# Chunk-selected attention with a gated MLP: score strips by query halves, PSUM tiles in pairs, dummy matmuls at the start, a new order table

## The chip, the core and the metric

The kernel runs on one core of one Trainium2 chip. A core has five queues of instructions that the profile names: PE (TensorE, matmuls; PEld are its weight loads), ACT (ScalarE), DVE (VectorE), POOL (GpSimd) and SP (SyncE, which issues transfers). Each queue is worked off in the order of the program, and queues wait for each other through semaphores. The metric is the time of one execution in device microseconds (us), given as the median of three runs.

## What is computed

The inputs are q, k and v (4 batches, 8 heads, 768 positions, 64 wide) and four weights of an MLP. Each query may look only at the 6 chunks of 32 keys with the largest upper bound of their scores, and only backwards.

```python
def _attn_ref(q, k, v):
    B, H, S, D = q.shape                       # 4, 8, 768, 64
    chunk = 32; nc = S // chunk; top_k = 6; scale = 1.0 / np.sqrt(D)
    k_chunks = k.reshape(B, H, nc, chunk, D)
    k_min = np.min(k_chunks, axis=3); k_max = np.max(k_chunks, axis=3)
    ub = np.sum(np.maximum(q[:, :, :, None, :] * k_min[:, :, None, :, :],
                           q[:, :, :, None, :] * k_max[:, :, None, :, :]), axis=-1)
    ub = np.where(causal, ub, -1000000000.0)
    top_chunks = np.argsort(ub, axis=-1)[..., -top_k:]
    scores = scale * np.matmul(q, k.transpose(0, 1, 3, 2))
    mask = sel & (pos[:, None] >= pos[None, :])
    scores = np.where(mask, scores, -1000000000.0)
    attn = np.exp(scores - np.max(scores, axis=-1, keepdims=True))
    attn = attn / (np.sum(attn, axis=-1, keepdims=True) + 1e-09)
    return np.matmul(attn, v)

def _moe_ref(x, w_in, w_spatial, b_spatial, w_out):   # x: (4, 768, 512)
    h = np.maximum(x @ w_in, 0.0)
    u, v = h[..., :512], h[..., 512:]
    v_n = (v - mean(v)) / np.sqrt(var(v) + 1e-06)
    v_s = np.einsum('ts,bsd->btd', w_spatial, v_n) + b_spatial[None, :, None]
    return (u * v_s) @ w_out
```

## The kernel before

**Units of work.** Two heads make a pair, and there are 16 pairs, four to a batch. A batch's MLP can begin when its four pairs are done. The 768 positions are six tiles of 128.

**A pair.** `load_ops` (L356) brings k, q and v; most loads are issued by POOL, which also turns them from f32 to f16 (L370), and some may go through SP into an f32 stage and a cast on an engine (L376). `prep_ops` (L431) turns k on PE (L440) or by a transfer (L443) into `kT`, takes minima and maxima per chunk on DVE (L449 to L455), turns q (L477), computes the bounds (`ub`, L489), picks the sixth largest (MAX8, L505) and writes the unselected chunks as extra rows beside q (`select`, L511). The result `qs` is turned into `a` by a transfer (L516) or on PE (L525). The extra rows of `kh` hold a large negative number, so one matmul gives scores with the chunk mask in them. The first pair has a path of its own, one head at a time (`prep_first`, L532: L545, L579, L590, L603, L616).

**Attention of a pair** (`attend_ops`, L623). Scores are computed transposed, keys by queries, in strips: for each key tile the queries from its diagonal on. `STRIPS` (L22) packs the 21 blocks of 128 by 128 of one head into six strips, five 512 wide and one 128 wide. Each strip takes a PSUM tile, PE fills it (L641), and ACT takes the exponential into `e` (L651). The three diagonal blocks of each half of the strips need a triangle set to zero: either PE adds a matrix of large negative numbers before the exponential (L644), or POOL clears them after it (L659). Then PE multiplies by v with a column of ones (L667), and DVE divides by the sum (L675, L679) into `x16`, which is turned into `xT` by a transfer (L687) or on PE (L694).

**The MLP of a batch** (`mlp_ops`, L700). Per tile of positions: four matmuls for v (L713), a ReLU, statistics and the normalisation on DVE (L719 to L730); four matmuls for u (L740) and a ReLU; six matmuls with the spatial weight (L754), a DVE instruction that adds the bias `bcol` and multiplies by u (L758) into `g`; `g` turned by a transfer (L762) or on PE (L768); four matmuls with `w_out` (L775), a copy into `o` (L240 on ACT or L244 on DVE) and a store (L780).

**What sets the order.** Operations are not issued in the order of the source. `Schedule.run` (L153) reads the string `PLAN` (L49): three digits name an operation, and the third also holds the engine, where an operation has several (`EVAC`, `RELU`, `KH` and so on), and which of eight PSUM tiles it takes. The table was found by a search outside the program; only its result is here. So one sequence holds the instructions of all engines, and each engine gets its share of it in this order. The semaphore waits are put in by the framework, from the tiles that each instruction reads and writes. The eight PSUM tiles are made one by one:

```python
    banks = [pp.tile([P, 512], F32, name=f"bank{j}") for j in range(8)]
    s = Schedule(banks, {"sc": 3, "tr": 2, "ub": 1, "av": 2, "mlp": 4})
```

Of the kernel before, what the change touches and what calls it, by code (L numbers as in the profile page):

```python
# [8 lines left out]
F32 = mybir.dt.float32  # L9
# [5 lines left out]
P = 128  # L15
# [5 lines left out]

STRIPS = [  # L22
    [(0, 0, 512, 0)],
    [(1, 128, 512, 0)],
    [(2, 256, 512, 0)],
    [(0, 512, 256, 0), (4, 512, 256, 256)],
    [(1, 640, 128, 0), (3, 384, 384, 128)],
    [(5, 640, 128, 0)],
]
WIDTHS = [512, 512, 512, 512, 512, 128]  # L30
BASES = [0, 512, 1024, 1536, 2048, 2560]
EW = 2688
DIAGS = [(0, 512), (1792, 384)]


def blocks(groups):
    out = []
    for g in groups:
        for (t, q0, n, col) in STRIPS[g]:
            for j in range(n // P):  # L40
                out.append((t, q0 // P + j, BASES[g] + col + j * P))
    return out
# [7 lines left out]
    "0700b00400000600100D00C00B00k00I00M00P00800c10J00H00500O10e00f10r40s10h00A00N11A82I00K10G00L10E0"  # L50
    "0l10Q01B03o00u00t01MC0w01D01010y00+11F03t02YG1C01H01J10i11E01N00302Z13w00v01L11G01O011K1K01I142O"
    "0200x00z11302o21205I02Q02N02b01PS0/114W4311Q08q00W02l12d00m04G11R05Y4AK05Q01504501S02c01602n21T8"
    "4JC2m24F24I25N05Z12pG1U12e017018K4601wO25S22W2f04702g02k04802h15b05c01z42r14A01912882j02701/02i0"
    "4902q00V01YK1tG4C02sS2A04L04E01g44B04D04K01v02401jC1a04M80X01l05e01VG2t01X05g02T01y01bW2u04N02v0"
    "4O094K2zS2xC2+01mG0F05d00R04P021O5f02y01d02C02D01i03TS4H19515pW5r03Y88y04T435C1o05h14RK3V04U03a0"
    "5q03GG8v09803I04S02/S9A03703Q42E03S05k05885i05j05sG5t09709C032W3104wCBq01fK5u03z09904y03N45A05v0"
    "52O5l16yS3P05406z01q03AC6q8AS05543406r03C04zO4/05700T05zG1r09B03bW3d05+04gS4i06oCAa85o11s03eO5x4"
    "3XG4jW3g04mK5n16bS5m15y1Ab0AP04o06p05T02F04l09LOAe03D84tC6e4Ad03i09E03F039K9N09D26QWAf06g00U03K0"
    "4v09G09F0DK09M09K16d09J14V8Ag09I14YOAh09H13j0Ai09O46YC3k06S04X0C4S6a03L09P06AG51W5C06C03M04a06NK"
    "9Q06T86P0ArC5/G6V05D0As19R09V45E06GOC509TW9W062K6I0Al0At0Aj065S6s8C804b49U0Am0Ap1Ak0AuCCA0610Av0"  # L60
    "6706XO3l06i04d0A5G6DWAw06409bS4f44q06j0Ax00S06F069KC704r0A8CAq19zW6t0A609c06K09+09YGDa8An19Z04s0"
    "9wSBv0By0A909e49f06k06L0Ao16uWC907IO78G9mCCC06M0Db09x0Ay09n0De05GKCB0CJ15H16m4CK16n0A0873S6+CDP0"
    "Gg0CL4CG2CF26v0A107906/0IA07J0CI0CE2CM1Dg0CH1700CN0ABK740Di07SWCD1Gl0CO8BG47K07T0750DS0Dd0Df07A0"
    "9jC090710AC0BDOCP0720BH08/0CQ09k07cS9pG7B0Jg07d0BeKBE09q06w4Bf0CR0760GwC7e0AV0B887C07NO7fG6x0B90"
    "7707U0BJKBK07O0Bb4Bc0CS0Dh0AD07L0Gx0Dl29g0Dn1Dj2B2SB307D07g07h07P1Dr8Go07iWDk10Y0BTKDs09r0BQCBR0"
    "9h4BhOBi07j0Dt0A20B5S7Q0BW87V0Dq1Dm0DuG7E07k19s09t0Gz09u07F0Dv07W0A3CAE0Dw0IF0Dp1CmOAF0BU07R0Do1"
    "CjKB60Dx07M07G0II0G/0CYW7rSBX0Cn0IS0D84Ck0AG07l87m0DV0H71BL0CbO7s0BA0CpKCZ07oWBj07n0CeG7H0H91DB8"
    "Cc07X07Y0DC07t07p0Dy0HA1Cf0Cq0BBOBM0BY0AICHB87q07b0H10CwSB/08MGHC07uKH81AJ17Z0BZWG+07a00Z0Bk0Jy0"
    "8N0H00BN0Jo07v0H20HD1Bl0H60BO0D5CD90H317w07x0Cx0D08IU0H40Cz4EGS82OH50If1Cg0Bm0Cr0D60D10E8CC+0D20"
    "HEKHF0E908O0Ih8LA0HG0EH0E548CWE60IW08D0Ij1HH0E2C8E0EWSE30Jl0Ii0IT0EJ4EK0Ig18F0EeKIV0Ef0Ch8EQCED4"  # L70
    "EhWDD0HI0EE0Cs08P0BoKIY0830IX0EX0OW0Ct0840Ib0ETG8W4ER0J+0IZ0EbSEU0Ia1Ic1Ei0Id2Ec0K00850Bp1D3CDE0"
    "Jz0DF0IkGIl0LQW8X07y0EA0EBOJ/0DG0Im0K208Q0EL0EM0KBSIn0LI08Y0Cu0Ie1LR1EN0860K108gCKC1EO0HZKLU0Io0"
    "8h0Ha0HsWHt0DIGEY0Hm8Hn08i0Ej0EZOKA1HUKEk0I1WHV0LF0K50RW0LT0KD1DJ1K718Z0Ev8Ob0K42I20K61K928a0K30"
    "El0Em0LV07/4OmKLW0HcOEoS8j0LY0Hd0Gr0Ep0K81HpGLX0Lc0KEC8TWE+SHfOE/0On0Ew0Oq0FIKHq0IL0F00FJ0Lb0Ex0"
    "Oe0KF08U0KG0FDGF10800FE0Op0LhSFK0JR8HOWHg0Ey0HR4EqKHP0Er0HS0F20J3OKH0JUCH+WIu4FF1La0Es1Q00JJGJ40"
    "Ez0FVKKI0Et0JV0Hh0810Iv0FW0H/0Li0Ld1JS0FX0FbOFc0Lj0LZ0HxCHu0Hy0Eu0Q80JX4JK0FL0Os0Ou0JY0IxSOr0LkW"
    "Iy08d8FG0FhKLe18G0Fi0Lf0J9CJA0Ll0Ot0Jr0F30JMGF84HW0F90J6SLg1JN0Lm0HXCHi0Ow2T00I30Fj1FA1HvGJGKFH0"
    "Hj08e0Ln0Ov2FB0F40F50K+8QI0I40J70JZ0Rb0P14P20P30Hk0Oy1Fd0I+W8JSJH0O/189OO+1Lo0Oz18A1K/0FC0P01Ro0"
    "FM0F60Ox0I508K0Re0JO0I/0KcKL18Kp4KmSL20J00Kd0P4CFYWKq0I60Kf8KxOFZ0FSKP50Kn0KO4Fa1FT0FeGKy0KP08k0"
    "KRSQ50P60P70JB0KZOJPWF70FU08B0Ja0Jb0Kg0FN0Ka0Jc0Ks4MGKFO0L+8Kt0KS0FkCFf0Fg0MROLuWMS0J14FQ0MH0JC0"  # L80
    "KUSFP0Fl0M9GGCOFR0LxKGD0KV0Ku0QU1P80QJ0L/0Kh0QV1Fm0I70LL0QK0MUSKW0JD0MM8Rp0JE0Rq0Fn0GE0MA0L30Lv0"
    "QL0MN0QM0QN0Fo0GF0Rr0Rs0MV0MX4MY0Jd0M3GQT1MZ0M6WFuCKv8L40KXSL50T50M70PE4PF0QO0PfOFv0MJWL60Fw0Ly0"
    "Fx0Rt0M40Oh08n88o1Fy0QX4Ki0Kj0PiKS02QZ0GMGMK0M00QY1PSCPPWQQ0QP1GN0QW1Kk0M18Pg0PT0T80PV4PW0Ru0TI0"
    "PHOPI0PtSQS0MB0GO0MC0MD0ME08L0L70PqCPK4Pu0QR1Pj0GP0MO0MPOMa0PL0GWSRx2QaKPn8G24Pr0Rw2M+GPcCMb0Po0"
    "Pd0Mc0Md0Pv0N8OGX0GY0S18Qb0G30G40Qc0Qd0S30TK0TV18V0Rv2Pk0Qe0PQ0Ry1GZ0FrCRh0MlKFs0TJ0S20TXWTY0MqS"
    "S48MgCM/0TM0S50TL0S60TZ1R/2Mh0N00TN0S70QB0TO0TP0TS0Mm0Mn1Mo0Mi0N90NA1F/WNXGPX0NY08p0S80GG0Qq8TU2"
    "TQ1G00Mp0QnCG50Mj0Qr0Mr0GQ0TR0Ms0QyKQz0PlWG10TaOTb0Qk8Mt0Tc0Td0Q/4Pw0Px0Mu0NZ0TT1TE0NLSQo0PM0Mk0"
    "NIKN3GN40N51N60Ql0RCCRD0NJ0R+2N70RN8RO0NK1G60R00NM0QvONN0PNCQs0Mv0PY0Py0Qw0SfGGJ8Sg0St4Su0ScSNUK"
    "GK1R6OGa0Rz0Te0Sd0N10NV0NRWNS0GL0TF0Mw0My0R70TC0SKGR10Ft0PZ0Pa0SP8SS4SQ0SL0SnSSo0NW1NOONP0SECSF0"
    "RK8NQ1RHGR9KQtSNB0RI0R20GTOSiCR30N20RA0Mx0R40SqGRL0GdKRE0NC0Sr0ND0Sj0RP0G98ST0GU18f0NE0Ge1TnSTo0"  # L90
    "GA0SVGMz0NF0RFOTqCOMKTW1U64SW0SHSSI0NT1RQ0Tr0Na8SM0Nb0TkGTl0Ts0UCWTySU70NkCUD0Nl0NG0Sk0NH0Pz0Nc0"
    "U9GTz0Sv0T/4RR0RS0Nm0UA0UNOSX0Nn0NuWRT0Nd0No0U00SNSSY0SZ0TD0UKGUL0UO0Ne0UH4SlCSw0Sa0Nv0Tv8O2GUI0"
    "UP0Sx0Sy0Tw0Sz0ON0OO0U10Nw0TtOVNSU20U30U40Gf0UE0UF4UQ0UR0US0Nx0Ny0NrCNs0OP0UW8O30UUOUg4UV1UqCUvW"
    "O40Uh0O50UbKU+OUi1U/0V00Uj0Uk0UX0VBGV10V20Nt0UY0Uc0UZ0GB0Uw0Ux1VH4VI0Ud0Ue0Ur0Us0Uf0Ua0Ut0Uu0Uy0"
    "VJ0VKOUl0VO0Um0VP0OC8NhKUz0O60Ni0V8WUn0N/CUo0OQ0V30V40V60V90OD0GV0V70V50VL0O94OA1VC0OB0VuSVQKOE0"
    "VE4O00VA0O10Up0Vv0VR0VS0OF0VT0OTCVD0VM0VaWVb0Vc0Vd0Nj0Vw0VkGOG0VF0Vl0Vx0OU0Vm0VU0OV0Ve0OJOVG1Vn0"
    "W28W30Vy0W40WCKWD0WE0VhCW50WF0OK0Vo0OL0VXWW60WHSV/4Vi0WI0Vj0VrGVY0W00VZ0W10Vs0Vt0WJOWK0WL0W98WA0"
    "WB0"
# [3 lines left out]
class Bank:  # L102
    def __init__(self, cls):
        self.cls, self.tile = cls, None
# [14 lines left out]
class Schedule:  # L119
# [3 lines left out]
    def __init__(self, banks, caps):  # L123
        self.ops, self.banks, self.caps = [], banks, caps
        self.keys, self.mode = {}, {}

    def op(self, alts, emit, key, r=(), w=(), take=None, drop=None, load=0.0, tag="", when=None, after=()):
# [66 lines left out]
def kernel(  # L194
# [40 lines left out]
    banks = [pp.tile([P, 512], F32, name=f"bank{j}") for j in range(8)]  # L235
    s = Schedule(banks, {"sc": 3, "tr": 2, "ub": 1, "av": 2, "mlp": 4})
# [34 lines left out]
    bcol = cp.tile([P, NQT], F32, name="bcol")  # L271
    w_in_sb = cp.tile([P, NDO, DFF], F16, name="w_in")
# [7 lines left out]
    stage_r = ring(8, [P, NQT, D], F32, "stage")  # L280
# [10 lines left out]
    e_r = ring(4, [P, EW], F16, "e")  # L291
    rec_r = ring(4, [P, NQT, 1], F32, "rec")
    x_r = ring(3, [P, NQT, 2, D], F16, "x16")
    xT_r = ring(3, [P, NDO, S], F16, "xT")
    vr_r = ring(11, [P, DH], F32, "vraw")
# [7 lines left out]
    o_r = ring(4, [P, DM], F32, "o")  # L303

    nc.scalar.preload_act_table_set("natural_log_exp_and_others")
# [9 lines left out]

    def preset(qs):
        nc.vector.memset(qs[:, :, 0, 0:D], 0.0)
        nc.vector.memset(qs[:, :, 1, D:P], 0.0)

    def const_ops():  # L320
        s.op(("DVE", 0.1, 0.2), lambda: nc.vector.memset(identity, 0.0), -100, w=["identity"])
# [21 lines left out]
        for j in range(len(kh_r)):  # L343
            for hi in range(2):
                s.op([("ACT", 0.72, 0.87), ("DVE", 0.45, 0.58)], lambda e, j=j, hi=hi: copy(
                    e, kh_r[j][D * hi:D * hi + D, hi, :], ex, False), -40 + 10 * j, r=["ex"], w=[("exrow", j, hi)])
        s.op(("SP", 0.45, 2.5), lambda: nc.sync.dma_start(out=bcol, in_=moe_b_spatial.rearrange("(t p) -> p t", p=P)),
             20, w=["bcol"])

    def both(qs):  # L350
# [479 lines left out]
```

## Time and profile before

| | |
|---|---|
| three runs | 197.38, 198.13, 1056.44 us |
| median | 198.13 us |
| the profiled execution | 195.9 us |
| its span, first to last instruction | 194.2 us |
| busy DVE, ACT, POOL | 158.4 (82%), 147.9 (76%), 118.5 us (61%) |
| first matmul of a score strip (L641) | starts at 16.00 us |
| last matmul (L775) | ends at 190.5 us |
| transposes by transfer | `gT` 23, `a` 11, `xT` 9, `kT` 5 |

The profiled execution is the one that durations are taken from. One of the three runs is far from the other two, and the median is not moved by it. A row of a group in the profile gives the line, the engine, the operation, output and input tiles with their shapes, the count, the busy time with the mean duration of one in ns, and the engine's idle time just before such instructions with what ended it. Matmuls follow each other in a pipeline: the mean duration of one includes the time until its result is written, and the time from one to the next is shorter. A busy PE is therefore not yet a PE at its peak.

### The profile page before, as it was taken

How to read it: one execution, taken by the hardware profiler on the slowest of the kernel's cores; microseconds unless marked ns; L12 is line 12 of the kernel's file. 1: busy time of each engine (PE TensorE's matmuls, PEld its weight loads, DVE VectorE, ACT ScalarE, POOL GpSimd, SP SyncE). 2: the span in 40 equal slices, each digit the busy share in tenths (PEclk: the TensorE clock that was granted, in tenths of full speed). 3: DMA queues.
4: the chain of work that ended last, by engine and by line, in shares of the span. 5: the costliest groups of instructions: out<-in, count | busy, mean ns of one | idle time of the engine just before them, and what ended most of it. 6: DMA issues, size and time to landing. Idle time of an engine off the chain costs nothing.

```text
span 194.2 us, 5292 instructions
## 1 busy us (share of the span) xinstructions
PE 181.0 (93%) x1888; PEld 112.8 (58%) x1888; DVE 158.4 (82%) x568; ACT 147.9 (76%) x317; POOL 118.5 (61%) x207
## 2 busy tenths in 40 slices
PE   0579999999998999999999999999999999999992
PEld 0367888776664657565566566555565664444440
DVE  8799999896999889998999986799889436973620
ACT  7799999989997999778989978667888722652142
POOL 7699999989999998697976785523223530000000
PEclk9999999999999999999999999999999999999999
DMA  6999999999999999999999999799994264406565
GB/s 133 137 160 171 192 167 146 137 149 171 155 155 168 125 119 175 124 172 146 201 139 150 203 108 150 187 142 222 149 265 65 41 149 137 110 0 199 139 203 216
DMA packets 122457, 29.50 MB, mean 152 GB/s; under 512 B 117056, under 2 KB 119360, under 8 KB 122432
## 3 DMA queue, kind: packets, MB, share of 16 engines
q0 software_dynamic: 72528, 11.60, 89.3%
q1 hardware_dynamic: 49904, 17.57, 48.6%
q8 instruction: 14, 0.23, 0.5%
q14 instruction: 11, 0.09, 0.2%
HBM read 24.38 MB, written 6.29 MB: 158 GB/s over the span
## 4 chain that ended last, share of the span: by engine, by line
PE 68%; DMA 12%; DVE 7%; ACT 5%; POOL 4%; issue 2%; SPq 1%; ACTq 0%; POOLq 0%; DVEq 0%
PE bank L754 13%; PE bank L641 13%; PE bank L775 10%; PE bank L740 9%; PE bank L713 8%; PE bank L667 7%; DMA a<-qs 4%; DMA qs<-in_q_dram 3%; DMA kp<-in_k_dram 3%; ACT e L651 2%; DMA stage<-in_k_dram 2%; PE bank L477 2%; DVE m L505 1%; PE bank L489 1%; DVE kmm L455 1%
## 5 line engine op out<-in xcount | busy, mean ns | idle before, releaser
L651 ACT ACTIVATE e<-bank 128x512 f16<-128x512 f32 (+1 forms) x192 | 92.4, 559 | 12.5 <-PE bank L641 9.8
L641 PE MATMUL bank<-a,kh 128*128 128x512 f16 (+3 forms) x256 | 56.1, 305 | 0.7 <-DMA a<-qs 0.7
L659 POOL TENSOR_SCALAR_AFFINE_SELECT e<-e 128x384 f16<-128x384 f16 x48 | 25.6, 550 | 22.0 <-ACT e L651 21.0
L754 PE MATMUL bank<-vn,wsT 128*128 128x512 f16 x144 | 38.0, 379 | 0.0
L641 PEld LDWEIGHTS <-kh 128*128 128x128 f16 x256 | 22.7, 97 | 15.8 <-DMA a<-qs 0.8
L667 PEld LDWEIGHTS <-e 128*128 128x128 f16 x672 | 25.4, 97 | 5.0 <-issue 0.3
L667 PE MATMUL bank<-vt,e 128*128 128x65 f16 x672 | 27.2, 193 | 0.2 <-ACT e L651 0.2
L242 POOL COPY kh<-kT 64x384 f16<-64x384 f16 x46 | 24.0, 522 | 3.7 <-PE bank L641 1.5
L758 DVE SCALAR_TENSOR_TENSOR g<-bank,bcol,u 128x512 f16<-128x512 f32 x24 | 17.6, 745 | 10.2 <-PE bank L754 10.0
L740 PE MATMUL bank<-w_in,xT 128*128 128x512 f16 x96 | 25.9, 379 | 0.0
L370 POOL DMA_DIRECT2D qs<-in_q_dram x30 | 25.1, 840 | 0.0
L713 PE MATMUL bank<-w_in,xT 128*128 128x512 f16 x96 | 24.4, 379 | 0.0
L240 ACT COPY o<-bank 128x512 f32<-128x512 f32 x18 | 10.4, 587 | 18.3 <-PE bank L775 18.3
L775 PE MATMUL bank<-w_out,gT 128*128 128x512 f16 x96 | 23.6, 379 | 0.0
L754 PEld LDWEIGHTS <-wsT 128*128 128x128 f16 x144 | 13.4, 98 | 12.1
L679 DVE TENSOR_TENSOR x<-bank,rec 128x384 f16<-128x384 f32 x32 | 17.5, 549 | 0.4
L370 POOL DMA_DIRECT2D kp<-in_k_dram x15 | 15.5, 1032 | 2.1 <-ACT qs L240 1.5
L719 DVE BATCH_NORM_STATS2 st<-vraw 128x6 f32<-128x512 f32 x24 | 16.3, 684 | 0.4
L370 POOL DMA_DIRECT2D vt<-in_v_dram x15 | 15.3, 1023 | 0.0
L775 PEld LDWEIGHTS <-gT 128*128 128x128 f16 x96 | 9.1, 98 | 9.7
L713 PEld LDWEIGHTS <-xT 128*128 128x128 f16 x96 | 9.0, 98 | 9.0
L740 PEld LDWEIGHTS <-xT 128*128 128x128 f16 x96 | 8.9, 98 | 8.5
(90 smaller groups left out, 280.0 us busy)
## 6 DMA issues: line engine op xcount, KB each, us to landing
out_dram<-o SPq DMA_DIRECT2D x24, 256.0 KB, 2.3
kp<-in_k_dram POOLq DMA_DIRECT2D x15, 192.0 KB, 6.1
qs<-in_q_dram POOLq DMA_DIRECT2D x30, 96.0 KB, 5.5
vt<-in_v_dram POOLq DMA_DIRECT2D x15, 192.0 KB, 6.5
ws_raw<-in_moe_w_spatial_dram POOLq DMA_DIRECT2D x3, 384.0 KB, 6.5
w_in<-in_moe_w_in_dram POOLq DMA_DIRECT2D x4, 256.0 KB, 7.8
w_out<-in_moe_w_out_dram POOLq DMA_DIRECT2D x2, 256.0 KB, 6.1
stage<-in_k_dram SPq DMA_DIRECT2D x2, 192.0 KB, 3.4
```

What stands on the lines that cost most here:

```text
L242: nc.gpsimd.tensor_copy(o, f)
L370: s.op(("POOL", cost, 0), lambda: nc.gpsimd.dma_start(out=o[0] if len(o) == 1 else o[2], in_=f[0] if len(f) == 1 else f[2]), key, w=w, loa ...
L641: mm(bs.f32[:, col:col + n], lhsT=kh[:, hi, t * P:(t + 1) * P], rhs=af[:, q0 // P:(q0 + n) // P, :], start=True, stop=not dg)
L651: s.op(("ACT", *act_cost(WIDTHS[g])), lambda g=g, bs=bs, e=e: nc.scalar.activation(out=e[:, BASES[g]:BASES[g] + WIDTHS[g]], in_=bs.f32[:, ...
L659: nc.gpsimd.affine_select(out=o, in_=o, compare_op=Alu.is_ge, fill=0.0, base=0, channel_multiplier=-1, pattern=[[0, 3], [1, P]])
L667: mm(o[:, qi, :], lhsT=e[:, c:c + P], rhs=vt[:, hi, t, 0:D + 1], start=(part == 0 and n == 0), stop=(part == 1 and n == len(bl) - 1))
L679: nc.vector.tensor_tensor(x16[:, :, hi, :], in0=o[:, :, 0:D], in1=rec.to_broadcast([P, NQT, D]), op=Alu.mult)
L713: mm(bk.f32, lhsT=x[:, ko, t * P:(t + 1) * P], rhs=w_in_sb[:, ko, DH:DFF], start=(ko == 0), stop=(ko == NDO - 1))
L740: mm(bk.f32, lhsT=x[:, ko, t * P:(t + 1) * P], rhs=w_in_sb[:, ko, 0:DH], start=(ko == 0), stop=(ko == NDO - 1))
L754: mm(bk.f32, lhsT=wsT[:, si, t * P:(t + 1) * P], rhs=vn[:, si, :], start=(si == 0), stop=(si == NQT - 1))
L758: s.op(("DVE", 0.67, 0.80), lambda t=t, bk=bk, g=g: nc.vector.scalar_tensor_tensor(out=g, in0=bk.f32, scalar=bcol[:, t:t + 1], in1=u_r[nu[ ...
L775: mm(bo.f32, lhsT=gT[:, db, :], rhs=w_out_sb[:, db, :], start=(db == 0), stop=(db == KO - 1))
```

## The change

The line numbers on the plus side are those of the changed kernel (`score` L672, triangle on PE L675, exponential L683, triangle by minimum on DVE L692 or POOL L694, multiplication with v L703, MLP L752, L779, L793, L797, L807, L814).

**PSUM tiles.** Four tiles of 1024 columns are made in place of eight of 512, and the eight entries that the table hands out are their halves:

```diff
-    banks = [pp.tile([P, 512], F32, name=f"bank{j}") for j in range(8)]
-    s = Schedule(banks, {"sc": 3, "tr": 2, "ub": 1, "av": 2, "mlp": 4})
+    double = [pp.tile([P, 1024], F32, name=f"bank{j}") for j in range(4)]
+    banks = [double[j // 2][:, 512 * (j % 2):512 * (j % 2) + 512] for j in range(8)]
+    s = Schedule(banks, double, {"sc": 3, "tr": 2, "ub": 1, "av": 2, "mlp": 4})
```

**Dummy matmuls.** A tile of zeros is multiplied with itself, 31 times and then three times 5; the groups are tied in before the first head's and the second head's transposes:

```diff
+        s.op(("DVE", 0.08, 0.15), lambda: nc.vector.memset(warm, 0.0), -102, w=["warm"])
+        for j in range(NWARM):
+            bw = Bank("tr")
+            def spin(n=31 if j == 0 else 5, bw=bw):
+                for _ in range(n):
+                    nc.tensor.matmul(bw.f32[:, 0:P], lhsT=warm, rhs=warm, start=True, stop=True)
```

**Score strips.** The 21 blocks of a head are packed so that strips 0 and 1 hold the queries of tiles 0 to 2, and strips 2 to 5 those of tiles 3 to 5. There are six strips as before. `e` becomes two rings of four, one for each half of the queries:

```diff
 STRIPS = [
-    [(0, 0, 512, 0)],
-    [(1, 128, 512, 0)],
-    [(2, 256, 512, 0)],
-    [(0, 512, 256, 0), (4, 512, 256, 256)],
-    [(1, 640, 128, 0), (3, 384, 384, 128)],
-    [(5, 640, 128, 0)],
+    [(0, 0, 256, 0), (2, 256, 128, 256), (0, 256, 128, 384)],
+    [(1, 128, 256, 0)],
+    [(0, 384, 384, 0), (5, 640, 128, 384)],
+    [(1, 384, 384, 0), (4, 512, 128, 384)],
+    [(2, 384, 384, 0), (3, 384, 128, 384)],
+    [(3, 512, 256, 0), (4, 640, 128, 256)],
 ]
-WIDTHS = [512, 512, 512, 512, 512, 128]
+HALF = [(0, 2), (2, 6)]
+WIDTHS = [512, 256, 512, 512, 512, 384]
+EW = [768, 1920]
```

**Triangles.** What POOL did may now also be done by DVE, as a minimum with a matrix of 0 and 60000:

```diff
+                    if eng == "DVE":
+                        nc.vector.tensor_tensor(o, in0=o, in1=tri_m.unsqueeze(1).to_broadcast([P, 3, P]), op=Alu.min)
+                    else:
+                        nc.gpsimd.affine_select(out=o, in_=o, compare_op=Alu.is_ge, fill=0.0, base=0,
+                                                channel_multiplier=-1, pattern=[[0, 3], [1, P]])
```

**Spatial bias.** It was loaded as 128 rows of six single numbers; now six rows of 128 are loaded and turned on PE:

```diff
-        s.op(("SP", 0.45, 2.5), lambda: nc.sync.dma_start(out=bcol, in_=moe_b_spatial.rearrange("(t p) -> p t", p=P)),
-             20, w=["bcol"])
+        s.op(("SP", 0.45, 0), lambda: nc.sync.dma_start(out=braw, in_=moe_b_spatial.rearrange("(t p) -> t p", p=P)),
+             -60, w=["braw"], load=0.1, tag="lb")
...
+        s.op(("PE", 0.25, 0.47), lambda: nc.tensor.transpose(bb.f32[:, 0:NQT], braw, idf), 20, r=["braw", "idf"], w=[bb], take=bb)
```

**Loads.** The way through SP and a stage is open only to k and q of the first pair. The built program uses it for one k and one q; before, it did so for two k, two q and two v.

**Buffers.** `stage` 8 to 4, `vraw` 11 to 9, `o` 4 to 3, `rec` 4 to 8.

**The table.** `PLAN` is replaced as a whole. The source also gains a way to treat a pair's query halves one after the other; with `SPLIT = 0` it is not used.

Instructions in the built program whose number changes:

| | before | after |
|---|---|---|
| PE score matmuls 512, 384, 256, 128 wide | 96, 32, 64, 64 | 0, 96, 96, 192 |
| PE dummies | 0 | 46 |
| PE transposes of k, x, g | 66, 42, 4 | 72, 30, 16 |
| ACT exponentials 512, 384, 256, 128 wide | 160, 0, 0, 32 | 128, 32, 32, 0 |
| triangles on POOL, on DVE | 48, 0 | 38, 10 |
| transposes by transfer of g, k, x | 23, 5, 9 | 20, 4, 11 |
| loads issued by POOL (k, q, v) | 15, 30, 15 | 16, 31, 16 |
| ReLUs and rq on ACT / on DVE (512 and 640 wide) | 40 / 42 | 50 / 32 |

## The prediction

> **What bounds the kernel now.** I read the page first: busy times, then the chain that ended last.
>
> ```profile
> span 194.2 us, 5292 instructions
> ...
> PE 181.0 (93%) x1888; PEld 112.8 (58%) x1888; DVE 158.4 (82%) x568; ACT 147.9 (76%) x317; POOL 118.5 (61%) x207
> ...
> PE   0579999999998999999999999999999999999992
> ...
> PE 68%; DMA 12%; DVE 7%; ACT 5%; POOL 4%; issue 2%; SPq 1%; ACTq 0%; POOLq 0%; DVEq 0%
> ```
>
> PE is busy from the third slice on and owns the chain. A busy PE need not be a full one, so I priced its work by the distance from one matmul to the next, from merged pieces of the chain and, for the transposes, of the timeline:
>
> ```profile
> 158.79 0.93 PE bank L667 x30
> ...
> 182.50 2.59 PE bank L754 x12
> ...
> 187.04 3.47 PE bank L775 x16
> 190.57 0.59 ACT o L240
> ```
>
> 12 matmuls 512 wide take 2.59 us: 0.216 each. The 65 wide ones take 0.031. Six transposes 128 wide at 36.56 take 0.49 with a last latency of 0.22: about 0.056 each. 256 and 384 wide lie between, 0.109 and 0.163; the 24 and 48 wide about 0.026 (ten in 0.41). Before: 528 of 512 (113.9), 32 of 384 (5.2), 64 of 256 (7.0), 422 of 128 (23.5), 672 of 65 (20.8), 170 narrow (4.4): **174.9 us of PE work**. The first score starts at 16.0, with 3.9 us of work behind it; PE ends at 190.5. So 171.0 us of work fill 174.5 us: after 16.0 PE loses 3.5 us in all. Whatever makes PE wait after the start goes into the time almost one for one. After PE come 3.7 us: the last copy and its store.
>
> The waits say the same:
>
> ```profile
> ACT e L651 <- PE bank L641: 9.8, 23, 1.1
> ...
> PE bank L641 <- DMA a<-qs: 0.7, 1, 0.7
> ...
> PE bank L667 <- ACT e L651: 0.2, 1, 0.2
> ```
>
> Others wait for PE; PE hardly waits for them, because a PSUM tile that it needs was emptied long before.
>
> The start, in the timeline of PE:
>
> ```profile
> 12.84 0.82 PE L440 MATMUL bank<-identity,kp 128*128 128x128 f16 x6 [0.74 <-DMA kp<-in_k_dram]
> 13.46 0.85 PE L616 MATMUL bank<-identity,qs 128*128 128x128 f16 x6
> 14.10 1.49 PE L477 MATMUL bank<-identity,qs 128*128 128x128 f16 x12
> 15.38 0.72 PE L616 MATMUL bank<-identity,qs 128*128 128x128 f16 x6
> 16.00 0.38 PE L641 MATMUL bank<-a,kh 128*128 128x512 f16 x1
> ```
>
> A k transfer issued at 7.41 holds the queue until 12.84, and six transposes take 0.82 here against 0.49 at 36.56.
>
> **The change part by part.**
>
> *PE work.* After: 432 of 512 (93.2), 96 of 384 (15.6), 96 of 256 (10.5), 556 of 128 without dummies (31.0), 672 of 65 (20.8), narrow 4.5: 175.6 us, 0.7 more. The new strips have the same columns, 128 more instructions (about 0.3), and g has 12 more transposes, x 12 fewer, k 6 more.
>
> *Start.* In the new order one k half is POOL's first load. Before the first score stand the k of pairs 1 and 2 and the q of pair 1; the k of pair 2 is POOL's fourth load, issued at about 4.2 (0.8 for the half, 0.8 for two selects, 1.0 for a k, 0.8 for a q, from 0.8 on), and 6.1 us to landing gives 10.3; the q of pair 1 follows at 6.0+5.5 = 11.5. Transposes, bounds and the copy of `a` run beside that. I take the first score at 12.5; bounds 11.5 (that landing) and 16.0 (no gain). Only 2.9 us of work lie before it, so 172.7 follow.
>
> *Dummies.* 36 at 0.107 (0.82 less latency, over 5) from about 1.0 end at 4.9, when the first k is cast (3.86+0.51 = 4.4): 0 to 0.5 us late, hidden by the landing above. They could also gain: 0.33 per group of six, four groups on the path, 1.3 at most; the landing decides, so I take 0. The row for the clock reads 1.00 in every stretch, though the durations double before 15.4. The Trainium skill (TensorE: Matmul & The Clock Gate, Part 1) explains such rows: the array starts at half rate, about 3.4 us of sustained work release it, and an idle window of that length throttles it again. By that rule the dummies end the slow time some 10 us sooner, worth the 1.3; the same rule speaks against them, because PE again waits between 5 and 10 us.
>
> *Exponentials.* 192 instructions and 86,016 columns before and after: 0. *Triangles:* ten of 48 go to DVE, between 0.40 (L449) and 0.55 us (L679), 4 to 5.5 us; with the moved ReLUs and copies DVE gains about 1 us, ACT 3, POOL loses 6. All have 36 us or more of idle time; uncovered it would be 1 to 3 us. *Bias:* one transpose (0.03) and a copy (0.1 to 0.2); g first needs it at 72.7, so 0. *SP's queue:* 35 compute transposes instead of 37 for g, k and x: 0. *Loads:* POOL issues three more (2.7 us) in an engine 61% busy; its 3.9 us wait for a staged v goes, off the path: 0. *Tail:* the last two g are turned on PE, each wait (0.75 for L758, 0.42 for the copy) under 0.86 of `w_out` matmuls; the `o` ring of three adds 0 to 0.6 where a store (2.3 to landing) is still out. I take 0.
>
> *PSUM pairs.* This part decides. The framework puts in waits by tile, and a tile now has two halves. In the built programs I followed each wait of PE on ACT or DVE to the instruction that releases it:
>
> ```
> released by a reader of    before: same half   other half     after: same half   other half
> PE waits on ACT                        256           -                   65          108
> PE waits on DVE                        138           -                   62           65
> ACT waits on PE / DVE              192 / 63         -              106 / 38      65 / 59
> DVE waits on PE / ACT              110 / 77         -               60 / 40      42 / 56
> ```
>
> So 173 times PE must wait for a read of columns it doesn't touch. How late is it? I added up the PE work that stands in the order between the reader and the waiting matmul. Before, its median is 1.6 us for ACT and 1.3 for DVE, and a read takes 0.61 (512 wide exponential), 0.55 (L679) or 0.75 (L758), plus about 0.05 to pass it on (ACT's cast ends at 6.31, PE starts at 6.36): done in time. After, for the other-half waits, the medians are 0.48 and 0.46, and in 70 of 173 it is below 0.3.
>
> Price: at each wait, duration less the work between, less what PE already lost since the reader. If a reader starts when PE comes to its place in the order, this adds up to 50.0 us over 123 waits after the first score, 34 of it other halves, the rest same-half waits that have also become short (19 ACT, 22 DVE). If every reader starts as soon as the matmuls that feed it are done (0.17 latency), 18.2 us over 45 waits. The same sums for before are 2.3 and 0.0, where the trace lost 3.5. In the trace of before ACT starts a median 0.15 us after PE reaches that place (5 to 95%: -0.02 to 0.55), which is nearest to 50.0; but in a longer span ACT's 151 us leave it freer to run ahead. I take **43**. The other-half waits of ACT and DVE (222) delay readers further: 0 if they are done in time, some 12 us at 0.05 each; I keep that for the range. Queued behind each such wait are all later matmuls, PE being in order.
>
> The Trainium skill (PSUM — Partial Sum Buffer, PSUM bank collisions) asks to guard PSUM by bank and says that accesses to different banks run clean. By that page the halves, banks of their own, need no such wait, and the sum would be the first rival's; no run here shows the chip without them, and the built program has them.
>
> **Sum.** 12.5 + 172.7 + 43 + 3.7 = 231.9 us of span. Before, the profiled execution lies 1.7 above its span and the median 2.2 above that: 231.9 + 3.9 = 235.8, so **236**.
>
> **Rivals.**
> - *The pair waits are hidden* and only the start counts: 12.5 + 172.7 + 3.5 + 3.7 = 192.4, median 196.3, not slower. For it: PE hardly waits now. Against: the work between reader and matmul has shrunk below a read's length in most cases. It decides if the 173 waits cost together less than 5.8 us (202.1, 2% above 198.13, less 196.3), 0.03 each. Chance 0.07: 0.05 within 2%, 0.02 faster, which needs the earlier start and almost no loss.
> - *The low price*: readers run ahead. 12.5 + 172.7 + 18.2 + 3.5 + 3.7 = 210.6, median 214.5; up to 222. For it: ACT idles a quarter of the span. Against: the 0.15 us above. Chance 0.19.
> - *The waits feed each other* through ACT and DVE: 50.0 + 12 + 3.5 with a first score at 14 make 255.9, median 259.8; from 252 on. For it: ACT and DVE now wait for each other's reads too (59 and 56). Chance 0.09.
> - *My forecast*, 222 to 252: 0.65.
>
> **Range and chances.** 212 to 255 takes in the forecast and most of the low price, and leaves out some 0.17. A measurement of this kernel tells about 2% from no change. Slower 0.93, same 0.05, faster 0.02.
>
> **What would show it.** In the changed profile: PE's idle before L672, L752, L779 and L793 ended by ACT or DVE lines, in sum 30 to 50 us, spread over the attention part and small in the last 35 us of PE work, where few such waits stand; mean durations unchanged (exponential about 610 ns at 512); the first score at 11.5 to 14; 3 to 4 us after the last matmul. Wrong: PE idle below 6 us after the first score, or idle that DMA or POOL ends; or a clock row below 1.00 while PE waits, which I haven't priced.

## The result and the profile after

| | before | after |
|---|---|---|
| median (lowest to highest) | 198.94 us (197.38 to 1056.44) | 274.45 us (274.13 to 275.32) |
| the profiled execution, its span | 195.9, 194.2 us | 275.3, 273.6 us |
| first score starts, last matmul ends | 16.00, 190.49 us | 15.57, 269.57 us |

Each kernel has four runs here, the kernel before one more (199.75 us) than stand ahead of the prediction; the ratio of after to before, 1.3838 with a 95% interval from 1.3725 to 1.3952, leaves out the run of 1056.44 us. The page of the changed kernel: span, busy times, PE and its granted clock in 40 slices, and the chain that ended last.

```profile
span 273.6 us, 5663 instructions
...
PE 209.8 (77%) x2069; PEld 130.7 (48%) x2069; DVE 163.7 (60%) x581; ACT 156.6 (57%) x330; POOL 112.8 (41%) x186
...
PE   8485687877767978577876797868687879899793
...
PEclk9669889999999988999997999989979999999999
...
PE 1%; ACT 0%; DVE 0%; issue 0%; ACTq 0%
```

The clock row of the kernel before, for comparison:

```profile
PEclk9999999999999999999999999999999999999999
```

No engine is full any more: PE falls from 93% to 77%, DVE from 82% to 60%, ACT from 76% to 57%. Their work has hardly changed; all three wait. (PE's busy time is higher than before, 209.8 against 181.0 us, because it counts the time until a result is written at each gap, and the matmuls at half clock; priced by distance its work is 1.65 us more.) PE has holes in almost every slice, and the clock row, which in the kernel before was full from 15.8 us on, has dents. The chain is of no use here: it could be followed for 1% of the span only, and shares that add up to 1% say nothing about the rest.

The waits (engine and line, what released them: us in all, times, longest):

```profile
PEld L672 <- issue: 28.1, 50, 1.7
ACT e L683 <- PE bank L672: 24.9, 35, 2.3
...
PEld L779 <- issue: 15.3, 24, 1.3
...
PE bank L779 <- ACT e L683: 7.8, 9, 1.2
...
PE bank L672 <- ACT e L683: 6.8, 12, 1.2
...
PE bank L752 <- ACT e L683: 3.0, 4, 1.0
...
PE bank L672 <- DVE rec L713: 3.0, 5, 1.6
```

PE now waits for the exponentials and for DVE, and the exponentials wait for PE. The view shows only a part of PE's loss. It counts idle time from the modelled end of the last matmul, 0.17 us after the moment at which the next one could have started, and "issue" names no releaser. So I matched the trace to the built program: each matmul's start less the start of the one before, less the price of that one, and the wait that ended last. Gaps below 0.03 us are left out.

| us after the first score | before | after |
|---|---|---|
| from first score to last matmul's end | 174.5 | 254.0 |
| PE work in it | 171.05 | 172.7 |
| lost | 3.4 | 81.3 |
| ... at waits for a reader of the other half | - | 55.1 in 83 gaps (ACT 33.2, DVE 21.9) |
| ... in all other waits (for a reader of the same columns, or for an input of the matmul) | 3.4 in 13 | 16.8 in 32 |
| ... at half clock | 0 | 8.3 |

DMA and POOL end none of these gaps in the changed kernel. Some 4.5 us in 7 of the 32 are waits for an input, such as `rq` (at 25.01 us, 1.6 us long). One stretch shows how the halves work on each other (timeline: start, us, engine, line, tiles; idle time before in brackets):

```profile
81.24 0.59 PE L779 MATMUL bank<-w_in,xT 128*128 128x512 f16 x2
81.87 1.09 ACT L683 ACTIVATE e<-bank 128x512 f16<-128x512 f32 x2 [0.90 <-PE bank L779]
...
82.52 0.38 PE L779 MATMUL bank<-w_in,xT 128*128 128x512 f16 x1 [0.69 <-ACT e L683]
```

In the built program the matmuls at 81.24 write the right half of the first PSUM tile, and the exponential at 81.87 reads its left half, whose matmuls had ended by 79.5. ACT stands idle for 0.90 us all the same, until the tile's last writer has ended. The next matmul writes the right half again and waits for that exponential to leave the left one. Both engines touch nothing in common, and take turns.

### The profile page after: what moved, and what is told of

Its sections match the earlier page's. It is cut to its first block, busy times and chain, and to the rows that moved or that the text cites. A ratio compares the mean times of both kernels' runs of the same rounds, so it can differ in the third digit from the quotient of the medians.

```text
span 273.6 us, 5663 instructions
## 1 busy us (share of the span) xinstructions
PE 209.8 (77%) x2069; PEld 130.7 (48%) x2069; DVE 163.7 (60%) x581; ACT 156.6 (57%) x330; POOL 112.8 (41%) x186
## 5 line engine op out<-in xcount | busy, mean ns | idle before, releaser
L683 ACT ACTIVATE e<-bank 128x512 f16<-128x512 f32 (+2 forms) x192 | 96.3, 545 | 59.9 <-PE bank L672 24.9
L672 PE MATMUL bank<-a,kh 128*128 128x128 f16 (+2 forms) x384 | 63.7, 268 | 23.5 <-ACT e L683 6.8
L672 PEld LDWEIGHTS <-kh 128*128 128x128 f16 x384 | 34.9, 101 | 46.2 <-issue 28.1
L694 POOL TENSOR_SCALAR_AFFINE_SELECT e<-e 128x384 f16<-128x384 f16 x38 | 19.4, 521 | 77.6 <-ACT e L683 76.9
L793 PE MATMUL bank<-vn,wsT 128*128 128x512 f16 x144 | 41.2, 392 | 3.3 <-DVE g L797 1.6
L779 PE MATMUL bank<-w_in,xT 128*128 128x512 f16 x96 | 29.3, 398 | 9.8 <-ACT e L683 7.8
L703 PE MATMUL bank<-vt,e 128*128 128x65 f16 x672 | 29.0, 196 | 5.5 <-DVE x L717 1.6
L703 PEld LDWEIGHTS <-e 128*128 128x128 f16 x672 | 26.7, 99 | 12.3 <-issue 7.1
L797 DVE SCALAR_TENSOR_TENSOR g<-bank,bcol,u 128x512 f16<-128x512 f32 x24 | 17.7, 746 | 19.3 <-PE bank L793 11.4
L752 PE MATMUL bank<-w_in,xT 128*128 128x512 f16 x96 | 26.1, 388 | 3.8 <-ACT e L683 3.0
L814 PE MATMUL bank<-w_out,gT 128*128 128x512 f16 x96 | 24.5, 379 | 1.2 <-ACT e L683 1.1
L793 PEld LDWEIGHTS <-wsT 128*128 128x128 f16 x144 | 13.0, 99 | 14.6 <-issue 5.4
L253 ACT ACTIVATE vraw<-bank 128x512 f32<-128x512 f32 x20 | 11.7, 596 | 13.7 <-PE bank L752 7.4
L779 PEld LDWEIGHTS <-xT 128*128 128x128 f16 x96 | 9.2, 102 | 19.8 <-issue 15.3
L398 POOL DMA_DIRECT2D vt<-in_v_dram x16 | 16.4, 1024 | 1.8 <-PE bank L703 1.4
L245 POOL COPY km<-kmm 64x24 f16<-64x24 f16 x20 | 4.4, 222 | 27.8 <-DVE kmm L483 21.8
```

Source lines behind the costliest of these rows:

```text
L245: nc.gpsimd.tensor_copy(o, f)
L398: s.op(("POOL", cost, 0), lambda: nc.gpsimd.dma_start(out=o[0] if len(o) == 1 else o[2], in_=f[0] if len(f) == 1 else f[2]), key, w=w, loa ...
L672: mm(bs.f32[:, col:col + n], lhsT=kh[:, hi, t * P:(t + 1) * P], rhs=a[:, f // P:(f + n) // P, hi, :], start=True, stop=not on)
L683: s.op(("ACT", *act_cost(n)), lambda g=g, n=n, bs=bs, e=e: nc.scalar.activation(out=e[:, BASES[g]:BASES[g] + n], in_=bs.f32[:, 0:n], func= ...
L694: nc.gpsimd.affine_select(out=o, in_=o, compare_op=Alu.is_ge, fill=0.0, base=0, channel_multiplier=-1, pattern=[[0, 3], [1, P]])
L703: mm(o[:, qi, :], lhsT=e[:, c:c + P], rhs=vt[:, hi, t, 0:D + 1], start=first and n == 0, stop=last and n == len(bl) - 1)
```

## The experiments

### The tiles alone, undone and done

**e1_eight_tiles:** the changed kernel with eight tiles.

```diff
-    double = [pp.tile([P, 1024], F32, name=f"bank{j}") for j in range(4)]
-    banks = [double[j // 2][:, 512 * (j % 2):512 * (j % 2) + 512] for j in range(8)]
-    s = Schedule(banks, double, {"sc": 3, "tr": 2, "ub": 1, "av": 2, "mlp": 4})
+    banks = [pp.tile([P, 512], F32, name=f"bank{j}") for j in range(8)]
+    s = Schedule(banks, None, {"sc": 3, "tr": 2, "ub": 1, "av": 2, "mlp": 4})
```

> The changed kernel with each PSUM bank a tile of its own again; the order and all other parts of the change stay. Theory A (waits for the other half cause the loss): the 83 gaps of 55.1 us vanish, most of the 16.8 us at same-half waits too (they came of delayed readers), and with PE busy the clock stays at 1.00: loss after the first score 3 to 8 us instead of 81.3. First score 15.6 + work 172.7 + 3 to 8 + tail 4.0 = span 195 to 200, time 197 to 204 (ratio to the kernel before 0.99 to 1.03). Rival B (the new order and strips are slow in themselves, whatever the tiles): at least 60 of the 81 us stay, time 253 or more. Rival C (half and half: 55.1 goes, the rest stays): about 219.

196.0 us, ratio to before 0.9944 (0.9913 to 0.9975): 1 us below theory A's 197 to 204, because the first score came at 13.2 us and not at the 15.6 that A had taken over. Its page:

```profile
span 194.5 us, 5638 instructions
...
PE 183.9 (95%) x2069; PEld 123.5 (64%) x2069; DVE 161.4 (83%) x581; ACT 150.4 (77%) x330; POOL 113.3 (58%) x186
...
PE   7588899999999799999999999999999999999991
...
PE 69%; ACT 13%; DVE 10%; DMA 5%; issue 1%; ACTq 0%
```

The same 2069 matmuls in the same order, with PE full again and owner of the chain. The loss after the first score is 4.5 us instead of 81.3. The windows from 30 to 40 us side by side, first of the changed kernel, then of this one (length, busy time and instructions of PE, PEld, DVE, ACT, POOL, clock, DMA share, GB/s):

```profile
30.00:40.00 10.00, 7.97 (x95) 6.56 (x95) 5.83 (x19) 5.22 (x14) 7.30 (x12) 0.83 0.99 69
```

```profile
30.00:40.00 10.00, 10.00 (x196) 9.41 (x193) 9.79 (x37) 9.86 (x23) 9.55 (x19) 1.00 1.95 174
```

In the same 10 us twice as many matmuls run, and PE, DVE, ACT and POOL are all above 9.5 us at once. The mean exponential of 512 columns takes 604 ns against 598: reading one bank while PE writes another costs nothing that can be seen. Theory A holds, and with it falls rival B: order, strips and the rest are not slow. Rival C falls too: the other waits (16.8 us) were for the most part a consequence, since all waits together lose 4.2 us here.

**e3_before_in_pairs:** the reverse, the kernel before with the pairs alone.

```diff
-    banks = [pp.tile([P, 512], F32, name=f"bank{j}") for j in range(8)]
+    double = [pp.tile([P, 1024], F32, name=f"bank{j}") for j in range(4)]
+    banks = [double[j // 2][:, 512 * (j % 2):512 * (j % 2) + 512] for j in range(8)]
```

> The kernel before with its eight PSUM banks as halves of four tiles; nothing else of the change. Theory A: the sum over its waits (duration of the reader less PE work between) is 51.2 us against 53.4 in the changed kernel, where 71.9 us were measured at waits and 8.3 at half clock; so some 48 to 80 us more than the kernel before: 247 to 280 us. Rival B: the pairs alone cost little, 198 to 205.

267.5 us (two runs: 267.1 and 267.9), ratio 1.3582 (1.3469 to 1.3695). PE loses 65.0 us at waits and 5.8 at half clock. The tiles alone, put into a kernel with the old order, the old strips and no dummies, cost 70 us, against the 78 that separate the changed kernel from e1.

**e2_other_pairs:** was the new table made for these pairs?

```diff
-    banks = [double[j // 2][:, 512 * (j % 2):512 * (j % 2) + 512] for j in range(8)]
+    banks = [double[j % 4][:, 512 * (j // 4):512 * (j // 4) + 512] for j in range(8)]
```

> The changed kernel with the eight banks paired in another way (bank 0 with 4, 1 with 5, and so on, instead of 0 with 1, 2 with 3). The order is the same. Theory A with an order made blind to the pairs: the same number of waits for other halves, so about the same loss; the sum over these waits that gives 53.4 us for the changed kernel (each wait: duration of the reader less PE work between) gives 51.5 here, so 264 to 285 us. Theory A with an order that was made to suit the pairs: clearly more than 285. Rival B: 274, unchanged, and the idle time of PE is not spread anew.

276.2 us (two runs: 275.2 and 277.2), ratio 1.4026 (1.3901 to 1.4151), within 1% of the changed kernel. So nothing shows that the order was made for the pairs it was given: another pairing costs about the same.

### How the price grows

My sum had come out too low, so two more kernels vary the number of banks in a tile, to tell two ways of pricing apart. Theory P takes PE's waits alone. Theory F follows PE, ACT and DVE through the built program, each in its own order, with the durations of e1's trace; each instruction starts when its engine is free and its waits are over, plus 0.05 us; reads that follow each other overlap by 0.13 us on ACT and 0.085 on DVE, as in the traces of before and e1. It was made when e1, e2 and e3 were known; e5 and e6 test it.

**e5_one_pair** and **e6_tiles_of_four:**

```diff
-    double = [pp.tile([P, 1024], F32, name=f"bank{j}") for j in range(4)]
-    banks = [double[j // 2][:, 512 * (j % 2):512 * (j % 2) + 512] for j in range(8)]
+    double = [pp.tile([P, 1024], F32, name="bank0"), pp.tile([P, 512], F32, name="bank1"), pp.tile([P, 512], F32, name="bank2"), pp.tile([P, 512], F32, name="bank3"), pp.tile([P, 512], F32, name="bank4"), pp.tile([P, 512], F32, name="bank5"), pp.tile([P, 512], F32, name="bank6")]
+    banks = [double[i][:, 512 * j:512 * j + 512] for i, j in [(0, 0), (0, 1), (1, 0), (2, 0), (3, 0), (4, 0), (5, 0), (6, 0)]]
```

and

```diff
+    double = [pp.tile([P, 2048], F32, name="bank0"), pp.tile([P, 2048], F32, name="bank1")]
+    banks = [double[i][:, 512 * j:512 * j + 512] for i, j in [(0, 0), (0, 1), (0, 2), (0, 3), (1, 0), (1, 1), (1, 2), (1, 3)]]
```

> The changed kernel with one pair of halves (banks 0 and 1) and six tiles of 512; the order and all else as in the changed kernel. Both theories start from e1_eight_tiles (196.0). Theory P (PE's waits alone: each is priced by the reader's duration less the PE work in between, the readers being on time): 13.5 us more than eight tiles, 208 to 212. Theory F (ACT and DVE also wait for the other half, PE's waits and theirs feed each other; followed wait by wait through the three engines with the durations of e1_eight_tiles): 18.6 us more at waits and up to 2 at half clock, 214 to 218.

218.4 us, ratio 1.1031 (1.0951 to 1.1112).

> The changed kernel with two PSUM tiles of four banks each; the order and all else as in the changed kernel. Theory P: 104.6 us more than eight tiles, 301, and at most 20 more at half clock: 300 to 320. Theory F: 165 us more at waits, 361, and 10 to 35 at half clock since PE is busy less than half of the time: 360 to 400.

413.9 us (two runs: 412.3 and 415.5), ratio 2.0903 (2.0737 to 2.1070). Its page:

```profile
span 413.8 us, 5690 instructions
...
PEclk9556555796956566985898699596769697799988
```

TensorE is at half clock for long stretches (5 and 6 in the row, 0.77 in the mean). What the kernels with shared tiles lost:

| us lost at waits after the first score | theory P | theory F | measured |
|---|---|---|---|
| eight tiles (e1) | 4.4 | 2.1 | 4.2 |
| one pair (e5) | 17.9 | 20.7 | 23.1 |
| before in pairs (e3, durations of its own trace) | 51.2 | 62.4 | 65.0 |
| the changed kernel | 53.4 | 69.1 | 71.9 |
| other pairs (e2) | 51.5 | 73.8 | 76.4 |
| tiles of four (e6) | 109.0 | 166.9 | 167.5 |

Theory F is within 3 us in every row; P is low by 5 to 59 in the five with shared tiles. In e6 the split of the loss is rough: if each matmul at half clock is charged its full extra time, 162 us remain at waits and 55 are half clock. Both e5 and e6 ended above the top of F's range, though: e5 by 0.4 us, e6 by 13.9, because half clock cost at least 42.3 us there, above the 10 to 35 allowed, and its first score came at 19.7 us, 6.5 later than in e1.

Followed with some waits left out, the changed kernel loses 31.7 us when ACT and DVE have no waits for the other half, 27.1 when PE has none, 2.7 when nobody has one, and 69.1 with all. That is worked out from e1's trace and the program. No run shows it: PE's and the readers' waits come from the same tile, and I found no kernel that has only one kind.

### Dummies and the clock

**e4_eight_tiles_no_dummies** (`def spin(n=0, bw=bw)` in e1) and **e10_pairs_no_dummies** (the same in the changed kernel). The prediction and the texts on these runs speak of 36 dummies; the program has 46, and both kernels leave out all.

> As e1_eight_tiles, without the 36 dummy matmuls; everything else alike. Theory (dummies worth nothing because the clock falls back to 0.50 at 8.5 us, before the transposes at 10): within 1 us of e1_eight_tiles, first score within 0.5 us of it. Rival (they still bring the full clock forward): 1 to 3 us slower than e1_eight_tiles, the clock 1.00 only some us later.

195.96 us, ratio 0.9958 (0.9927 to 0.9989); first score at 13.19 us, against 13.20 with dummies. The half rate lasts until 17.4 us here, while in e1 the clock is full from 5.3 to 8.7 and again from 12.1 us on; the last matmul starts at 189.97 us against 189.99. So the clock differs and the time doesn't.

> The changed kernel, pairs and all, without the 36 dummy matmuls. Theory (they bring nothing, since the clock falls back before the transposes): 273 to 276, the changed kernel took 274.5. Rival (in pairs the start is slower, because TensorE waits more and the clock comes back late): 276 to 280.

275.4 us, ratio 1.3971 (1.3907 to 1.4034); the changed kernel's 274.45 was measured beside other runs, and 0.9 us is too little to tell them apart.

**e9_fill_the_gap:** e1 with more of them, where TensorE stands still.

```diff
+        def bias():
+            nc.tensor.transpose(bb.f32[:, 0:NQT], braw, idf)
+            for _ in range(36):
+                nc.tensor.matmul(bb.f32[:, P:2 * P], lhsT=warm, rhs=warm, start=True, stop=True)
-        s.op(("PE", 0.25, 0.47), lambda: nc.tensor.transpose(bb.f32[:, 0:NQT], braw, idf), 20, r=["braw", "idf"], w=[bb], take=bb)
+        s.op(("PE", 0.25, 0.47), bias, 20, r=["braw", "idf"], w=[bb], take=bb)
```

> As e1_eight_tiles, with 36 more dummy matmuls right after the transpose of the spatial bias, where TensorE otherwise stands still from 6.6 to 8.7 us. Clock, theory H (in the rows so far the clock of a 3.41 us stretch fell to 0.50 when TensorE was busy for less than about 0.37 of the stretch before, and came back only after a stretch of about 0.78 or more): the stretch up to 8.7 us is now some 0.9 busy, the clock stays at 1.00 through the transposes at 9 to 12 us, and six of them take 0.49 us instead of 0.80 to 0.85. Rival: only an unbroken run of work counts, it falls as before. Time, theory S (ACT's chain of copies and bounds, and DVE, set the start, not TensorE): within 0.5 us of 196.0. Rival: the transposes are on the path, 1.0 to 1.5 us less, 194.5 to 195.0.

196.1 us, ratio 0.9934 (0.9906 to 0.9962). The timelines of PE, of e1 and then of e9:

```profile
8.97 0.80 PE L467 MATMUL bank<-identity,kp 128*128 128x128 f16 x6
9.56 0.85 PE L606 MATMUL bank<-identity,qs 128*128 128x128 f16 x6
...
12.52 0.41 PE L617 MATMUL bank<-kmf,rq 128*128 128x24 f16 x10 [0.83 <-ACT rq L252]
```

```profile
8.92 0.49 PE L471 MATMUL bank<-identity,kp 128*128 128x128 f16 x6
9.25 0.50 PE L610 MATMUL bank<-identity,qs 128*128 128x128 f16 x6
...
12.49 0.41 PE L621 MATMUL bank<-kmf,rq 128*128 128x24 f16 x10 [1.47 <-ACT rq L252]
```

The clock stays full and six transposes take 0.49 instead of 0.80 us, as theory H had it. But the bounds at 12.5 us wait for ACT's `rq` in both, and PE's gain turns into a longer wait (1.47 for 0.83 us). A TensorE at full clock brought nothing here, where another engine's chain sets the start.

### Triangles and bias

**e7_triangles_on_pool** (e1 with `if False:` in place of `if eng == "DVE":`).

> As e1_eight_tiles, but the ten triangles that the changed kernel gives to DVE go to POOL, so all 48 stand there. Theory (covered on either engine): 196.0, within 0.5 us of e1_eight_tiles. Rival (POOL is late with them and ACT, PE wait for `e`): 1 to 3 us more.

197.8 us, ratio 1.0006 (0.9973 to 1.0039): the rival. Its waits show where:

```profile
PEld L702 <- POOL e L693: 1.4, 2, 1.2
```

At two places PE waits for a triangle on POOL, a line that e1 does not have, and PE's loss rises from 4.5 to 6.0 us. So the ten triangles on DVE are worth some 1.8 us, no less than the eight-tile version gains on the kernel before (0.56%, 1.1 us). The two ratios come from separate comparisons and their intervals just touch; but e8, which differs from e1 in the bias alone and ran beside e7, took 196.2 us.

**e8_bias_by_columns** (e1, but the DMA writes `bcol` by columns, and the copy of the identity, transpose and copy issue nothing).

> As e1_eight_tiles, but the spatial bias is read by columns as in the kernel before (one DMA straight into `bcol`), without the copy of the identity, the transpose and the copy of the result. Theory (bias worth nothing): within 0.5 us of 196.0. Rival: the DMA by columns held SP's queue 1.09 us before and the one by rows 0.48, so the transfers behind it on SP and with them the first score come up to 0.6 us later, 196.6.

196.2 us, ratio 0.9928 (0.9879 to 0.9977), first score at 12.96 us. No difference that can be told, and the start is not later.

## Why the prediction was wrong

The direction was right, and so was the cause, waits for the other half of a tile; their price was not. The time lies 38 us above the forecast and 19 above its range.

| term | predicted | measured |
|---|---|---|
| first score | 12.5 (11.5 to 16.0) | 15.57 |
| PE work after it | 172.7 | 172.7 (priced the same way) |
| PE's losses | 43 (18.2 to 50.0, and up to 12 more) | 81.3 |
| after PE | 3.7 | 4.05 |
| span | 231.9 | 273.6 |
| median above the span | 3.9 | 0.9 |

- **The step that failed** is the price of PE's losses, taken as 43 us: "If a reader starts when PE comes to its place in the order, this adds up to 50.0 us", and beside it, as a sum of its own kept for the range, "0 if they are done in time, some 12 us at 0.05 each" for the waits of the readers themselves. The changed kernel lost 81.3 us: 71.9 at waits, 8.3 at half clock and 1.1 in small gaps. Followed through the three engines (theory F) the waits come to 69.1 us, and to 2.7 without any for the other half. PE's own waits alone make 29.0 of that difference, less than I had priced them; the readers' alone make 24.4, where I had 0 to 12; and 13.0 come on top when both stand: a reader held back by the other half's writer starts later, PE waits longer for it, and its next matmul holds back the next reader. So the mis-sized term is the readers' waits, and the two kinds do not simply add. This split is worked out, not measured; the runs show the total.
- I read "in a longer span ACT's 151 us leave it freer to run ahead" as a reason to go below 50.0. It did not run ahead. Measured from the place in the order at which the matmul before has streamed, an exponential started a median 0.14 us late before and 0.10 in the changed kernel, and the late ones became later: 5 to 95% went from -0.02 to 0.53 us to -0.18 to 0.70. The 0.15 us that I leaned on came from a kernel whose readers had no such waits.
- **The third rival**, waits that feed each other, named what happened. Its 259.8 us stopped short because it added the same separate sums, and had no clock.
- **The clock** was the unpriced risk, named as a sign of being wrong: 8.3 us. Its five falls to 0.50 after the start (at 32.4, 100.7, 145.1, 182.6 and 199.7 us) came after stretches in which TensorE streamed for 0.28, 0.30, 0.20, 0.14 and 0.36 of the time.
- **Start.** With eight tiles the first score comes at 13.2 us, 0.7 after my value. ACT sets it, not the landing of q: in e1 ACT works without a gap above 0.03 us from 3.59 us until its copy of `a` ends at 13.15. The other 2.4 us are pair waits ahead of the first score (e10: 15.6 without dummies). The lines are from e1:

```profile
12.37 0.78 ACT L242 COPY a<-bank 128x768 f16<-128x768 f16 x1
...
13.20 0.27 PE L671 MATMUL bank<-a,kh 128*128 128x256 f16 x1
```

- **Dummies at 0**: right (e4, e10), also when they keep the clock up (e9). The 1.3 us that the transposes could gain were gained on PE and hidden.
- **Bias at 0**: right (e8). **Triangles at 0**: wrong once the tiles are undone (e7), in the bounds of 1 to 3 us that I gave for lost cover. With pairs it was not tried.
- **The first rival's sum**, 192.4 us of span and 196.3 median with the pair waits hidden, is close to what e1 gives when they are gone: 194.5 and 196.0. That the medians agree within 0.3 us is luck in part: the span was 2.1 us longer, and the median lies 1.5 us above it, not 3.9. The Trainium skill (PSUM — Partial Sum Buffer, PSUM bank collisions) had said that accesses to different banks run clean; e1 is the run that lacked at the time.
- **Signs.** Idle time of PE ended by ACT and DVE, little in the last 35 us of PE work: 5.0 us of the 81.3 fall there. The groups' idle time before L672, L752, L779 and L793 adds to 40.4 us on the page (45.9 with L703), inside the 30 to 50 that I had asked for. As a sign it was misleading: 0.17 us at each of 115 gaps, 20 us, are not in it. The sign at the start failed: a first score at 11.5 to 14 was asked for, and it came at 15.57.

What stays open: in e1 the first score is 2.8 us earlier than before and the last matmul ends at the same time, since 1.65 us more work and 1.0 us more loss follow; its median still lies 1.8 us lower than that of the kernel before beside it. The profile of the kernel before is one of its quickest executions: its span is 194.2 us, and the median span of its 23 runs beside e1 is 195.5, against 194.3 for e1's 12. In which part of the kernel that 1.2 us arises, no profile shows.

The best version found is the change with eight tiles (e1), 0.56% faster than before (0.25 to 0.87%); e4, e8 and e9 are the same within their intervals. That is far below the 2% that the prediction called tellable; it rests on four kernels whose intervals all lie below 1.

## What to carry to other kernels

Make each PSUM bank a tile of its own wherever waits are put in by tile: tiles over two banks cost 78 of 274 us here, with the same work on every engine. Price a new kind of wait by following all engines that have it, not one engine with the others on time; where waits run both ways, the sum over one engine's waits was low by a quarter with pairs and by a third with tiles of four. Before speeding up an engine at the start, look at what its first useful instruction waits for.

## What the runs showed of the hardware

The granted clock moves in stretches of 3.41 us. For each stretch in twelve profiles I added up the time in which TensorE streamed (each matmul for its recorded duration less 0.17 us) and looked at the clock of the next one. Stretches ahead of a run's first clock record count as at half rate. At full clock, all 44 stretches with a share below 0.33 were followed by 0.50, and none of 644 with 0.40 or more; between them 7 of 33. At half clock, none of 55 below 0.74 was followed by 1.00, and all 40 of 0.82 or more were; between them 15 of 18. So in these runs two thresholds keep the clock apart, and a TensorE that is half busy stays at whichever it has. e9 tested it: a gap filled, a clock kept.

The Trainium skill (TensorE: Matmul & The Clock Gate, HAM oscillation — how this bites in real kernels) puts it as no idle gaps above some 3.4 us. Here the clock of e1 fell at 8.71 us although the longest distance between two matmuls of the stretch before was 2.28 us; the share of the stretch decided, not the gap.

A clock row is to be read with care at the start: in e4 it says 1.00 from 10 to 15 us, while six transposes take 0.80 to 0.85 us. The first record of that run is at 17.4 us, and a stretch without records is shown as full. The window of e4 from 10 to 15 us (in the order of the windows above) and its transposes:

```profile
10.00:15.00 5.00, 4.17 (x41) 3.45 (x40) 4.84 (x22) 4.89 (x11) 4.88 (x8) 1.00 1.95 138
```

```profile
9.99 0.85 PE L467 MATMUL bank<-identity,kp 128*128 128x128 f16 x6
10.63 0.85 PE L643 MATMUL bank<-identity,qs 128*128 128x128 f16 x6
...
12.60 0.80 PE L504 MATMUL bank<-identity,qs 128*128 128x128 f16 x6
```
